# New constants in the scheduler's account of latencies, and new marks per score tile, in a fused attention and GLU kernel

## The chip, the cores and the metric

The kernel runs on one core of a Trainium2 chip. The metric is the device time of one execution in microseconds (us); lower is better. Durations of single instructions are given in nanoseconds (ns). The engines are PE (TensorE: matrix multiplications, with PEld for its weight loads), DVE (VectorE), ACT (ScalarE), POOL (GpSimd) and SP (SyncE, which issues most DMAs). Each engine has its own list of instructions, and semaphores make it wait for the others.

## What is computed

One transformer block over 2048 tokens of width 512: layer norm, attention with 32 heads of 16 dimensions, a residual, a second layer norm, a gated feed-forward network of inner width 1792, and a second residual. All inputs are bf16.

```python
def _A_ref(x, wqkv, wo):                       # H = 32, Dh = 16, S = 2048, D = 512
    q, k, v = split(x @ wqkv)
    scores = jnp.einsum("bhqd,bhkd->bhqk", q, k) * (Dh ** -0.5)
    p = _softmax(scores, axis=-1)
    o = jnp.einsum("bhqk,bhkd->bhqd", p, v)
    return merge_heads(o) @ wo

def _B_ref(x, w_gate, w_up, w_down):           # F = 1792
    h = _sigmoid(x @ w_gate) * (x @ w_up)
    return h @ w_down

h  = x + _A_ref(_layernorm(x), A_wqkv, A_wo)
h2 = h + _B_ref(_layernorm(h), B_w_gate, B_w_up, B_w_down)
```

## The kernel before

**Three stages.** A prologue (about 21 us) loads x, makes its layer norm and the first keys and queries. The main stage (21 to 753 us) runs attention, and squeezes all the other work that can already be done between the pieces of attention: the remaining projections, the output projection, and the feed-forward network of all token blocks but the last. A tail (753 to 783 us) does the last block's output projection and feed-forward network.

**Score tiles.** Attention is cut into 2048 units: 512 columns of scores for one head and one block of 128 keys. Three units make a tile (the last has two), so there are 683 tiles. For tile `n`, PE writes the transposed scores into one of two PSUM buffers `pss` (line 1119, three matmuls, or six of half the width). ACT turns them into bf16 exponentials in one instruction (`pt`, line 1503). Since there are two `pss` buffers, the scores of tile `n` can't begin before the exponentials of tile `n-2` are finished.

**Splitting a tile.** In many tiles ACT takes only two of the three units (128x1024 instead of 128x1536). DVE takes the third: it writes a 16-bit integer code `J` that, read as bf16, is an approximate exponential (line 1298), and for every four such units makes three shifted codes (`code`, line 1318, 128x2048), whose average is more exact. A unit on ACT is multiplied with the values once. A unit on DVE is multiplied four times, with `J` and with each of its three codes. These products (called AV below) accumulate in `acc` (line 1272); four of them, for four heads, run side by side in four column groups of PE, and such a group of four over 512 columns is called a round.

**Background work.** Everything else on PE is queued in `bg` as generators which each yield a few matmuls (`pe(2)` is two rounds' worth): value, key and query projections (`prep_v`, `prep_k`, `prep_q`), the output projection (`wo_add`), the feed-forward network (`ffn_up`, `ffn_down`). They write the one buffer `pm`, which ACT (`th`, the tanh of the gate, line 983) or DVE (`hT`, line 967, and others) empties before the next step can write it. If nothing fits and PE has done little for a while, `fill` issues a matmul whose result nobody reads (line 712).

**The scheduler.** The order of the main stage is not written out by hand. While the program is built, a loop keeps an account of when each engine will be free (`T["P"]`, `T["A"]`, `T["D"]`, `T["G"]`), and always lets the engine with the earliest time choose its next piece: `pe_step`, `act_step`, `dve_step`, `gps_step`. Each choice adds an assumed cost and notes when others may use the result. These costs are constants: a round on PE 217.5 ns (`MM`), the scores of a tile 214 ns (`SMM`), going into and out of score matmuls 105 and 116 ns (`S_IN`, `S_OUT`), 51 + 426.5 ns per unit on ACT, a hop between engines 100 ns (`LAT`), and a few offsets which tell how much later than its slot a result is complete. Only the order goes into the program: the hardware never sees the constants. It waits for semaphores, so a wrong constant makes no wrong result, only an order whose waits fall elsewhere than the account says.

**Marks.** Three strings of 683 letters (`MARKS`, a letter per tile and engine) bend the rules at single tiles. For ACT, `x` forbids to split this tile, `j` allows more work waiting on DVE, `o` gives DVE the first unit and not the last, `l` lets a group of codes stay open longer. For PE, `w` and `v` allow 150 ns more or less before the next scores, `p` presses AV forward, `f` puts background work first, `r` and `R` change how full AV rounds must be, `a` and `b` take or give credit for background work. For DVE, `s`, `e` and `c` shift its priority between `J`, other jobs, and codes.

In `pe_step`, PE may take AV or background work only while it fits before the next scores are due:

```python
act_end = max(T["A"], last_sc + LAT if e < s else T["A"])
limit = act_end + (s - e) * 905 - 520 if s < N else 1e12
room = limit - t + {"w": 150, "v": -150}.get(way, 0)
```

Of the kernel before, what the change touches and what calls it, by code (L numbers as in the profile page):

```python
# [10 lines left out]
BF16 = mybir.dt.bfloat16  # L11
# [12 lines left out]
CODE_STEP = (55, 93, 24)  # L24
MARKS = {
    "A": (
        "........x.oo.xoxxol....ojjoj.x.ooo....x.x....oxx..........j.jj...........o.x"
        "x.o.......xx.lj.jlljjj.xox..ooxjojj.j..x.j..x..j....ooo..ooooooj.x..jjj.jj.."
        "....jj...jjj...lol.....j..j..o....llll.jl...lll..o..............j..x..xx...."
        "jjjjj.jjjj.j..xxx.....j..o.....x...j.......x.ll..........................llj"  # L30
        "jjjjj.xo...llll.......xxx..j..o.j..............j.j.x.j........x.l..........x"
        "..............jj..xxo.j..oooo.ooo....oo......xooo....l..lllj.....x...l.....x"
        ".....lllllll.j.l.j.......jjjjlllll....xo.....j.jjjjjj.......l..oololoooo.x.x"
        "x..o...llll.x........o.jjjj..........l..........l.ll.lll...lllxljjl...j.jj.."
        "...llllxl..........xxoo....jjjjj.lx....j..........j.jx.xxxxx.o.ooooo.xx...l"
    ),
    "P": (
        "............aRR.ww........vww..p.p.pr........pp......f..ffR..a.a.aa..va..p.p"
        "p....vvvv.vvvbb....v.vf.a.bw........................f......p.p...vvvvvv.pvbb"
        ".b...........b.b.a...R.ppp.bR.r....b........pRRp.p..............wRRR.vvvvrr."  # L40
        "...rrp............f.br.v.vvvvv....pf........f....bb.....bb.bb..appp.aaa..pR."
        "aRp.a..v.v...p............wbww.wp.f......v.vvRv.vv.R.vpv..f.ffffafpp........"
        ".v.........RR...........RR..w...fff.ffv....p..........pvp..r..pprwrvr..brr.R"
        "Rrr.p.........f..aaaaaa..vvv...........vv..fvvvvr....f...f.ff.rpp...R......."
        "...............rrr...RR.ffR........brp.....ff...vvv.vvvv.w....v.wwp.....pp.p"
        ".r.......ab..a..pppwb..p...rf...........pffrr.R......rfffv.RRf.r...w...frrr"
    ),
    "D": (
        "....c..................cc...ee....s..........................c..c..........."
        ".c..sssssss..eeeeeee..e...ss..ssss..................c...c.e.ss.............."  # L50
        "....c.s........c.eec.ssss..........ccsssss.ss...ss................e........."
        ".....c.ccscc.....cccsssc.ecc.c.........c.......ee...eeeee.eee..ss..........."
        "....................e.................s.........eeee..s..............cc.scc."
        "........c......ee.ee......c.e...c...........cc......eeee...........sc......."
        "........es...................................c...sss.e.......c.............."
        "c............ssssss...........eeeeees..........s..................s.c......."
        "....s.......e.c.c.c.c.......ee....................c.....ss.sc..........c..."
    ),
}

# [1 line left out]
def kernel(  # L62
# [12 lines left out]
    P = 128  # L75
    S, D = A_x.shape[1], A_x.shape[2]
# [200 lines left out]
    V, A, E = nc.vector, nc.scalar, nc.tensor  # L277
# [132 lines left out]
    def center0(key, a, b, out):  # L410
# [5 lines left out]
        out=small.tile([P, 1], FP32, name="warm")[:], in_=eps_t[:], func=ACT.Sqrt))])  # L416
# [8 lines left out]
    for c in range(NQC):  # L425
# [40 lines left out]
        out=small.tile([P, 1], FP32, name="warm")[:], in_=eps_t[:], func=ACT.Exp))])  # L466

    def qproj0():
# [39 lines left out]
    while left:  # L508
        best = None
        for n in left:  # L510
            t = tasks[n]
# [20 lines left out]
        t = tasks[n]  # L532
# [155 lines left out]
                        moved = True  # L688

    MM = 217.5  # L690
    SMM, S_OUT, S_IN = 214.0, 116.0, 105.0
    FILL = 2000.0
    SPAN = 3413.0
    FROOM = 200
# [358 lines left out]
    def try_bg(tokens, loose=60.0):  # L1053
        while bg and bg[0][2] is None:
            advance()
        if not bg:
            return 0
        ns, mm, deps, mode = bg[0][2]
        ends = [d.end for d in deps if d is not None]
        if None in ends:  # L1060
            return 0
        r = max(ends, default=-LAT) + LAT
        if mm == 0:
            st["mark"] = None
            advance()
            return try_bg(tokens, loose)
        if tokens < mm or r > T["P"] + loose:
            return 0
        T["P"] = max(T["P"] + switch(mode), r) + ns
        st["work"] = "b"  # L1070
        worked(ns)
        st["mark"] = Mark(T["P"])
        bg[0][3] -= mm
        advance()
        return mm
# [32 lines left out]
    def scores(n):  # L1108
        for k in queries(n):
            force(k)  # L1110
        pss = ps_s.tile([P, GU, QC], FP32, name="pss")
        first = True
        for a in range(2):
            for ui, (q, g, kt, j) in enumerate(tiles[n]):
                hg = head_groups(q, g)
                if a >= len(hg):
                    continue
                w = QC // len(hg)
                mm = nc.tensor.matmul(  # L1119
                    pss[:, ui, a * w:(a + 1) * w],  # L1120
                    lhsT=KT[hg[a]][32 * j:32 * j + 32, kt * P:(kt + 1) * P],
                    rhs=(QT0[q] if q < NQC and g == 0 else QT[hg[a]])[32 * j:32 * j + 32, columns(q, a)],
                    start=True, stop=True, tile_position=(32 * j, 0))
# [26 lines left out]
    def finish_group(q, g):  # L1150
# [29 lines left out]
        def turn():  # L1180
# [111 lines left out]
    def dexp_first(src, un):  # L1292
        if not half:
            half.append(dvx.tile([P, NJ, QC], U16, name="J", bufs=NJB))
            first_codes.append([1])
        J, held = half[0], first_codes[-1]
        k = len(half) - 1
        first = nc.vector.tensor_scalar(out=J[:, k, :], in0=src, scalar1=128 * SC * LOG2E,  # L1298
                                        scalar2=float(CODE_BASE), op0=ALU.mult, op1=ALU.add)
        half.append(un)  # L1300
        held[0] += 1
        avq.append(Unit(un.u, J[:, k, :].bitcast(BF16), un.n, T["D"] + 680, held))
        prior["op"] = J
        if k == NJ - 1:
            dexp_rest()
        return first

    def dexp_rest():
        J, uns = half[0], half[1:]
        half.clear()  # L1310
        k = len(uns)
        j = J[:, 0:k, :]
        mine = first_codes[-1]
        mine[0] += NCODE - 1

        def code(i):
            c = dvx.tile([P, NJ, QC], U16, name="code", bufs=CB)[:, 0:k, :]
            nc.vector.tensor_scalar(out=c, in0=j, scalar1=CODE_STEP[i], scalar2=None, op0=ALU.add)  # L1318
# [138 lines left out]
    def act_step():  # L1457
# [24 lines left out]
        if (len(tl) == GU and len(jq) < 2 and mark("A", n) != "x"  # L1482
# [12 lines left out]
            elif can and back <= EASY:  # L1495
# [6 lines left out]
        pt = ptp.tile([P, GU, QC], BF16, name="pt")  # L1502
        ex = nc.scalar.activation(out=pt[:, lo:lo + wa, :], in_=pss[:, lo:lo + wa, :],  # L1503
                                  func=ACT.Exp, scale=SC)
# [198 lines left out]
```

## Time and profile before

| | us |
|---|---|
| median of three runs (lowest, highest) | 785.53 (784.61, 785.80) |
| the profiled execution's own time | 784.84 |
| its span, from first to last instruction | 782.8 |
| first and last start of an exponential (line 1503) | 21.0 and 751.6 |
| PE busy, PEld busy | 756.6 and 374.8 |
| ACT busy | 755.1 |
| DVE busy | 720.3 |
| PE clock granted | 1.000 throughout |

Two things need care when these are read. A busy share counts the time in which at least one instruction of the engine was in flight. Instructions of one engine overlap: an exponential of two units lasts 1018 ns or more from its start to its end, but when ACT is fed well the next one starts 904 ns after it. Short waits thus vanish under the overlap, and ACT at 100% busy in the main stage may still be waiting. The distance from one start to the next shows them; sums below are therefore made of such distances and not of durations. And the median of the runs lies 0.69 us above the profiled execution.

### The profile page before, as it was taken

The numbers are of one execution on the slowest core, as the hardware profiler recorded it, in microseconds if no ns is written. First come the engines' busy times: TensorE is split into PE (matmuls) and PEld (weight loads), VectorE is DVE, ScalarE is ACT, GpSimd is POOL, SyncE is SP. The second block draws the span as 40 slices with busy tenths as digits, with TensorE's granted clock in tenths as the row PEclk, the third lists the DMA queues.
The fourth block names the chain that finished last, engine by engine and source line by source line (L and its number), as shares of the span: only waits on it lengthen the run. The fifth ranks groups of instructions, "written<-read, shape, count | busy, mean of one in ns | idle before, by whom it ended". The sixth has DMA issues, their size and how long they took to land.

```text
span 782.8 us, 34032 instructions
## 1 busy us (share of the span) xinstructions
PE 756.6 (97%) x15274; PEld 374.8 (48%) x15274; DVE 720.3 (92%) x1339; ACT 755.1 (96%) x786; POOL 47.4 (6%) x124
## 2 busy tenths in 40 slices
PE   8999999999999999999999999999999999999998
PEld 7423323444455534554455434554554355544656
DVE  6999999999999999999998999999999999999652
ACT  7999999999999999999999999999999999999972
POOL 2000000000110001000100001001000010000000
PEclk9999999999999999999999999999999999999999
DMA  6503022236013320221023310320133113223510
GB/s 200 122 2 76 2 50 48 58 72 179 16 30 82 85 63 15 71 84 57 15 58 90 90 43 26 109 82 11 37 97 90 56 41 92 84 63 102 155 34 21
DMA packets 93810, 52.99 MB, mean 68 GB/s; under 512 B 21520, under 2 KB 92576, under 8 KB 93664
## 3 DMA queue, kind: packets, MB, share of 16 engines
q1 hardware_dynamic: 92848, 50.56, 23.5%
q8 instruction: 119, 1.95, 1.0%
q10 hardware_dynamic: 816, 0.26, 0.1%
q14 instruction: 27, 0.22, 0.1%
HBM read 39.52 MB, written 2.11 MB: 53 GB/s over the span
## 4 chain that ended last, share of the span: by engine, by line
ACT 42%; PE 30%; issue 13%; DVE 12%; POOL 1%; DMA 1%; SPq 0%; ACTq 0%; DVEq 0%
ACT pt L1503 40%; PE pm L214 10%; PE acc L1272 8%; PE pss L1119 8%; DVE J L1298 5%; DVE code L1318 4%; ACT th L983 2%; PE gu L209 2%; PE hp L1673 1%; DMA code<-in_A_x_dram 1%; DVE qd L815 0%; DVE xs L1205 0%; PE acc L209 0%; DVE ob L977 0%; DVE h L932 0%
## 5 line engine op out<-in xcount | busy, mean ns | idle before, releaser
L1503 ACT ACTIVATE pt<-pss 128x1024 bf16<-128x1024 f32 (+1 forms) x683 | 716.7, 1212 | 1.8 <-PE pss L1119 1.1
L1298 DVE TENSOR_SCALAR J<-pss 128x512 uint16<-128x512 f32 x501 | 332.2, 681 | 10.4 <-PE pss L1119 9.8
L1119 PE MATMUL pss<-QT,KT 32*128 32x256 bf16 (+1 forms) x3584 | 269.3, 288 | 16.3 <-ACT pt L1503 10.7
L1318 DVE TENSOR_SCALAR code<-J 128x2048 uint16<-128x2048 uint16 (+3 forms) x399 | 249.9, 658 | 0.7
L1272 PE MATMUL acc<-pt,Vaug 128*17 128x256 bf16 (+1 forms) x2701 | 233.6, 290 | 0.3
L1272 PE MATMUL acc<-code,Vaug 128*17 128x256 bf16 (+1 forms) x2649 | 197.2, 288 | 0.1
L1119 PEld LDWEIGHTS <-KT 32*128 32x128 bf16 x3584 | 89.3, 92 | 209.2 <-issue 109.1
L1272 PEld LDWEIGHTS <-Vaug 128*17 128x17 bf16 x6233 | 137.4, 90 | 101.3 <-issue 81.6
L1272 PE MATMUL acc<-J,Vaug 128*17 128x256 bf16 (+1 forms) x883 | 144.0, 288 | 0.1
L214 PE MATMUL pm<-xT,wgu 128*32 128x256 bf16 x3136 | 116.2, 274 | 1.1 <-DMA wgu<-in_B_w_gate_dram 0.4
L214 PEld LDWEIGHTS <-wgu 128*32 128x32 bf16 x3136 | 76.6, 96 | 27.0 <-issue 23.8
L214 PE MATMUL pm<-wd,hT 128*32 128x512 bf16 x728 | 53.2, 383 | 0.3 <-DVE h L932 0.3
L967 DVE SCALAR_TENSOR_TENSOR hT<-th,pm 128x512 bf16<-128x512 f32 x49 | 33.3, 680 | 13.2 <-PE pm L214 12.7
L1171 POOL TENSOR_TENSOR o<-xs,rec 128x256 bf16<-128x256 f32 x23 | 16.2, 706 | 391.9 <-DVE rec L1167 391.9
L983 ACT ACTIVATE th<-pm 128x512 f32<-128x512 f32 x49 | 33.6, 685 | 0.0
L1205 DVE STREAM_TRANSPOSE xs<-acc 128x512 f32<-128x512 f32 x32 | 22.7, 711 | 6.0 <-PE acc L1272 5.8
L214 PEld LDWEIGHTS <-hT 128*32 128x32 bf16 x728 | 14.3, 95 | 17.8 <-issue 13.4
L214 PE MATMUL pm<-xT,wk_sb 128*32 128x512 bf16 x256 | 19.5, 383 | 0.1
L214 PE MATMUL pm<-xT,wq_sb 128*32 128x512 bf16 x256 | 19.5, 383 | 0.1
L214 PE MATMUL pm<-wo_sb,ot 128*32 128x512 bf16 x224 | 17.3, 383 | 0.7 <-DVE hT L967 0.5
L214 PE MATMUL pm<-wv_sb,xT 128*32 128x448 bf16 x256 | 17.5, 356 | 0.0
L1177 POOL TENSOR_TENSOR o<-xs,rec 128x256 bf16<-128x256 f32 x8 | 5.3, 660 | 187.3 <-DVE rec L1167 187.3
(155 smaller groups left out, 347.4 us busy)
## 6 DMA issues: line engine op xcount, KB each, us to landing
wgu<-in_B_w_gate_dram SPq DMA_DIRECT2D x49, 256.0 KB
wgu<-in_B_w_up_dram SPq DMA_DIRECT2D x49, 256.0 KB
KT<-half_neg SPq DMA_DIRECT2D x7, 512.0 KB
QT<-qd SPq DMA_DIRECT2D x28, 128.0 KB
KT<-kd SPq DMA_DIRECT2D x7, 256.0 KB
wd<-in_B_w_down_dram SPq DMA_DIRECT2D x1, 1792.0 KB
xr<-in_A_x_dram SPq DMA_DIRECT2D x14, 128.0 KB
out_dram<-ob SPq DMA_DIRECT2D x14, 128.0 KB
```

What stands on the lines that cost most here:

```text
L209: nc.tensor.matmul(ps, lhsT=lhsT, rhs=rhs, start=start, stop=stop)
L214: nc.tensor.matmul(ps[r, :], lhsT=lhsT[:, r], rhs=rhs, start=start, stop=stop, tile_position=(0, 32 * j), skip_group_check=True)
L967: nc.vector.scalar_tensor_tensor(out=hT[:, 2 * k:2 * k + 2, :].rearrange("p f q -> p (f q)"), in0=th[:], scalar=1.0, in1=ps, op0=ALU.add, ...
L983: nc.scalar.activation(out=th[:], in_=ps, func=ACT.Tanh, scale=0.5)
L1119: mm = nc.tensor.matmul(pss[:, ui, a * w:(a + 1) * w], lhsT=KT[hg[a]][32 * j:32 * j + 32, kt * P:(kt + 1) * P], rhs=(QT0[q] if q < NQC and ...
L1171: V.tensor_tensor(out=o2[:, 0:NB, :].rearrange("p b (a d) -> p a b d", a=2), in0=xs[:, :, 0:DH].rearrange("p (a b) d -> p a b d", a=2), in ...
L1205: j = st["acc"] = dve(630, lambda: nc.vector.transpose(out=xs[:].rearrange("p b r -> p (b r)"), in_=acc[:]), Mark(T["P"]))
L1272: nc.tensor.matmul(acc[32 * j:32 * j + VW, a * w:(a + 1) * w], lhsT=Vaug[:, kt, 4 * hg[a] + j, :], rhs=un.ap[:, a * w:(a + 1) * w], start= ...
L1298: first = nc.vector.tensor_scalar(out=J[:, k, :], in0=src, scalar1=128 * SC * LOG2E, scalar2=float(CODE_BASE), op0=ALU.mult, op1=ALU.add)
L1318: nc.vector.tensor_scalar(out=c, in0=j, scalar1=CODE_STEP[i], scalar2=None, op0=ALU.add)
L1503: ex = nc.scalar.activation(out=pt[:, lo:lo + wa, :], in_=pss[:, lo:lo + wa, :], func=ACT.Exp, scale=SC)
L1673: nc.tensor.matmul(ps, lhsT=hT[:, f, i * P:(i + 1) * P], rhs=wd[:, f, a:b], start=apart and f == 0, stop=(f == FC - 1), skip_group_check=True)
```

## The change

Two parts. The first replaces constants of the account:

- `S_OUT` and `S_IN` go from 116 and 105 ns to 113 and 97.
- The scores of a tile are held to be complete 185 ns after PE's slot, not 165 (`sc_end`).
- The exponentials are held to be complete 66 ns after ACT's slot, not 31, and ACT's slot is 16 ns longer when ACT had to wait.
- Results of background matmuls and of `acc` are held to be complete 115 or 175 ns after PE's slot, where nothing was added before (`st["mark"]`, and the transposition of `acc`).
- `J` is held to be complete 40 ns earlier than before, and a code 35 ns earlier.

The second replaces the three strings of marks: 322 of 683 letters differ for ACT, 352 for PE, 160 for DVE. The kernel's functions, tiles, buffers and formulas stay as they are; what the program executes changes only through the order that the scheduler now chooses, and through which tiles it splits.

```diff
 MARKS = {
     "A": (
-        "........x.oo.xoxxol....ojjoj.x.ooo....x.x....oxx..........j.jj...........o.x"
+        ".....xjj.jo..xoxxooo.oo.jjoj.x.o..x..xooo.....xx.....ooo....jj.......l...j.x"
...
     "P": (
-        "............aRR.ww........vww..p.p.pr........pp......f..ffR..a.a.aa..va..p.p"
+        ".......ff...vRR.ww........vww..p..a..RRR....p......v.a.vaafffa.wpa....a...ww"
...
     "D": (
-        "....c..................cc...ee....s..........................c..c..........."
+        "...e.e...........cc....cc...ee..........c......ce.c..........c..c..........."
...
-    SMM, S_OUT, S_IN = 214.0, 116.0, 105.0
+    SMM, S_OUT, S_IN = 214.0, 113.0, 97.0
...
-        st["mark"] = Mark(T["P"])
+        st["mark"] = Mark(T["P"] + (175 if bg[0][1][0] in ("f", "ln") else 115))
...
-        sc_end[n] = T["P"] + 165
+        sc_end[n] = T["P"] + 185
...
         j = st["acc"] = dve(630, lambda: nc.vector.transpose(
-            out=xs[:].rearrange("p b r -> p (b r)"), in_=acc[:]), Mark(T["P"]))
+            out=xs[:].rearrange("p b r -> p (b r)"), in_=acc[:]), Mark(T["P"] + 175))
...
-        avq.append(Unit(un.u, J[:, k, :].bitcast(BF16), un.n, T["D"] + 680, held))
+        avq.append(Unit(un.u, J[:, k, :].bitcast(BF16), un.n, T["D"] + 640, held))
...
-            avq.extend(Unit(un.u, c[:, m, :].bitcast(BF16), un.n, T["D"] + 85, held)
+            avq.extend(Unit(un.u, c[:, m, :].bitcast(BF16), un.n, T["D"] + 50, held)
                        for m, un in enumerate(uns))
...
-        T["A"] = start + 51 + 426.5 * wa
-        uns = [Unit(u, pt[:, ui, :], n, T["A"] + 31) for ui, u in enumerate(tl)]
+        T["A"] = start + 51 + 426.5 * wa + 16 * (start > t)
+        uns = [Unit(u, pt[:, ui, :], n, T["A"] + 66) for ui, u in enumerate(tl)]
         if split:
             jq.append((n, pss[:, pick, :], uns.pop(pick), ex))
         else:
-                    ex_end[n] = T["A"] + 31
+                    ex_end[n] = T["A"] + 66
```

More of the change, by code (lines that the diff above doesn't have):

```diff
@@ L26 @@
     "A": (
-        "........x.oo.xoxxol....ojjoj.x.ooo....x.x....oxx..........j.jj...........o.x"
[L28 to L32, printed above, removed]
@@ L33 @@
-        ".....lllllll.j.l.j.......jjjjlllll....xo.....j.jjjjjj.......l..oololoooo.x.x"
-        "x..o...llll.x........o.jjjj..........l..........l.ll.lll...lllxljjl...j.jj.."
-        "...llllxl..........xxoo....jjjjj.lx....j..........j.jx.xxxxx.o.ooooo.xx...l"
+        ".....xjj.jo..xoxxooo.oo.jjoj.x.o..x..xooo.....xx.....ooo....jj.......l...j.x"
+        "..oloooooooox..jj..jjjjjox..xxxxoxjlooojoj...x.lllll.ll..jx...ljooo.jjl.ll.."
+        "x...ll.jj..............jjllll..j..oxll.jl...lllj.j........x.oooljj..jjjjl..."
@@ new lines @@
+        "jjjjj.jjjj.j..xxx.o..lllj.jjjjjjxxjj.......x.ll..l...o.x......x..o.oo...l.lo"
+        "ooooooo.....lll...xo.o.oo.o.l.......olll.lox....l..x.j..l....ox.l.l........o"
+        "..xjl.........jjl.jj.j...oj...xo..ooo...ool..joool..xlllloo.o.o.l.llol...jj."
+        "o..oo...llll.j.l.lxl.oj.xxjjj..lll.....x.....xx....jjl.ll.jjj..ojj.....o...x"
+        "x......l.......ooooo.lljljx.oj....xll.....jj.j.jj..j.jjjj.llllxl.jl..jjoo..."
+        ".......oooooooojjo.xxoo.jj.jjjjj.l..ox.ll...j.l........ojjj.jjjjo.oo.x.x..."
@@ L36 @@
     ),
     "P": (
-        "............aRR.ww........vww..p.p.pr........pp......f..ffR..a.a.aa..va..p.p"
[L39 to L43, printed above, removed]
@@ L44 @@
-        "Rrr.p.........f..aaaaaa..vvv...........vv..fvvvvr....f...f.ff.rpp...R......."
-        "...............rrr...RR.ffR........brp.....ff...vvv.vvvv.w....v.wwp.....pp.p"
-        ".r.......ab..a..pppwb..p...rf...........pffrr.R......rfffv.RRf.r...w...frrr"
+        ".......ff...vRR.ww........vww..p..a..RRR....p......v.a.vaafffa.wpa....a...ww"
+        "wwwwwfvvaa.vpppp.vv.R.RfR.brrRr....rr.p.....ffffff.rrrr..rrpR.p....aa.a.aaav"
+        "pb...RR.b.b..b.b.p...R......vrRrRw.pp.vv....vRfvrpp...........bbRR.Rva.vvr.f"
@@ new lines @@
+        "f.rr.......vvv....fpbr.vvvvvv.v..rpf........r.r..bb...wpww.bb.ppaaw.pRR..pf."
+        "....fpp.prR.......R.ffww.pb..v..p.f......vrrrrv..www.v.v..f....vvvvvvbRR..aw"
+        "wwwff.ff...vv..p............wva...wwwfRrbbvb......p........r..fvvvpva.r...aa"
+        "....pv.....wpppp...p.r...vpv............aw.bbww..w...f..f.ppp.......R.R.aa.b"
+        "b.f.rrrrrrrv...rw.w.www..p....a..a...aav....ff...ffr.aa....rppv.ffff.bf....."
+        "vv..r....a.Rvvv.vvp.pbb.R.v.v......r........RRv..rr..rfff..a..a...vv...frrr"
@@ L47 @@
     ),
     "D": (
-        "....c..................cc...ee....s..........................c..c..........."
[L50 to L54, printed above, removed]
@@ L55 @@
-        "........es...................................c...sss.e.......c.............."
-        "c............ssssss...........eeeeees..........s..................s.c......."
-        "....s.......e.c.c.c.c.......ee....................c.....ss.sc..........c..."
+        "...e.e...........cc....cc...ee..........c......ce.c..........c..c..........."
+        ".c..s.ssssseee.e..ceeeee.ees..sseee........e.eeeeee.cee.........s..........."
+        "...sc.s........c.e.....s...........ccsssss.ss...ss...........c.cc.ccc......."
@@ new lines @@
+        ".....c.ccscc..eee........e.c.c.........c..eee..c.ccc..ceeeeee..c.....c.....e"
+        "ee.ee..c.c........e.e.....c.cc....................ece.s..............ce.scc."
+        ".s......c......e.cce......c.e.e.c.ccc.e.....c.c.c.e.ee.ce...cc......c......."
+        "......ccc...cccc..c....e.............ee......e...............c.......s......"
+        "c............cessss..eeecc....eee.ees.e........s.s................s.c......."
+        "....scccc...e.......c.......ee.c..........e.......c..ccccccs...sse.....c..."
```

## The prediction

> **What bounds the kernel now.** I read the page's busy times first, then the groups by form, then the timeline of single engines.
>
> ```profile
> PE 756.6 (97%) x15274; PEld 374.8 (48%) x15274; DVE 720.3 (92%) x1339; ACT 755.1 (96%) x786; POOL 47.4 (6%) x124
> PEclk9999999999999999999999999999999999999999
> ACT 42%; PE 30%; issue 13%; DVE 12%; POOL 1%; DMA 1%; SPq 0%; ACTq 0%; DVEq 0%
> ```
>
> Three engines are nearly full, and the chain of waits changes hands between ACT and PE. Which of them sets the pace must be read from distances between starts.
>
> ```profile
> L1503 ACT ACTIVATE pt<-pss 128x1024 bf16<-128x1024 f32 x502 | 489.1, 1101 | 1.7 <-PE pss L1119 1.1
> L1298 DVE TENSOR_SCALAR J<-pss 128x512 uint16<-128x512 f32 x501 | 332.2, 681 | 10.4 <-PE pss L1119 9.8
> L1503 ACT ACTIVATE pt<-pss 128x1536 bf16<-128x1536 f32 x181 | 263.5, 1520 | 0.0
> L1318 DVE TENSOR_SCALAR code<-J 128x2048 uint16<-128x2048 uint16 x354 | 233.2, 689 | 0.6
> L1119 PEld LDWEIGHTS <-KT 32*128 32x128 bf16 x3584 | 89.3, 92 | 209.2 <-issue 109.1 <-DVE J L1298 67.9 <-DVE code L1318 7.7
> ```
>
> 502 tiles are split and 181 are not. The means (1101, 1520 ns) contain overlap and waits; ACT's timeline gives the net times (start, length, instruction, count):
>
> ```profile
> 729.09 0.61 ACT L983 ACTIVATE th<-pm 128x512 f32<-128x512 f32 x1
> 729.58 4.15 ACT L1503 ACTIVATE pt<-pss 128x1536 bf16<-128x1536 f32 x3
> 733.57 0.65 ACT L983 ACTIVATE th<-pm 128x512 f32<-128x512 f32 x1
> ...
> 738.69 4.95 ACT L1503 ACTIVATE pt<-pss 128x1024 bf16<-128x1024 f32 x5
> 743.51 0.62 ACT L983 ACTIVATE th<-pm 128x512 f32<-128x512 f32 x1
> 743.99 4.66 ACT L1503 ACTIVATE pt<-pss 128x1024 bf16<-128x1024 f32 x4
> 748.45 0.69 ACT L983 ACTIVATE th<-pm 128x512 f32<-128x512 f32 x1
> ```
>
> Three unsplit tiles from 729.58 to 733.57 are 1.330 us each. The four from 743.99 to 748.45 are two unsplit and two split ones (the merged row names the first form only): (4.46 - 2.66)/2 = 0.90, and the commonest distance behind a split tile is 0.904. A tanh takes 0.477. Five split tiles should take 4.52 us from 738.69, but the tanh behind them starts 4.82 later: 0.30 us of waiting that no idle column shows. PE shows why:
>
> ```profile
> 737.67 0.39 PE L1119 MATMUL pss<-QT,KT 32*128 32x256 bf16 x6
> ...
> 738.54 0.39 PE L1119 MATMUL pss<-QT,KT 32*128 32x256 bf16 x6
> ...
> 739.30 1.05 PE L214 MATMUL pm<-xT,wgu 128*32 128x256 bf16 x30
> 740.28 0.39 PE L1119 MATMUL pss<-QT,KT 32*128 32x256 bf16 x6
> ```
>
> From one tile's scores to the next PE needs 0.436 us plus 0.2175 for each round: 0.87 with two rounds (737.67 to 738.54), 1.74 with six (738.54 to 740.28). Six rounds in one go outlast the buffer of two tiles.
>
> The main stage from the first exponential at 21.0 to the end of the last at 752.7 is 731.7 us. ACT's net work is 502 x 0.904 + 181 x 1.330 + 49 x 0.477 = 717.9, so it waits 13.7 us. Single distances put 11.5 us of that into 83 waits of over 50 ns, and in all but seven of these the scores came late because PE was still busy, not because DVE still read the buffer. Up to tile 200 PE has room: 191 us of work against ACT's 207, with 3.1 us of waits. From there to the last scores ACT has 509.7, PE 477 x 0.436 + 5 x 0.218 (scores following scores directly) + 1339 rounds x 0.2175 = 500.3, with 10.4 of waits. So ACT sets the pace, with PE 1.9% behind it.
>
> **The change part by part.** I compared the two built orders, instruction by instruction.
>
> *ACT.* 508 tiles are split instead of 502. Each further split takes 1.330 - 0.904 = 0.426 us from ACT: 6 x 0.426 = -2.56 us. By stretch: tiles 0 to 199 lose one split (+0.43), the rest gain seven (-2.98), four of them in the last 33 tiles. There DVE has room: the unsplit run at 729 to 738 shows its `hT` step idle before it for 3.83 us.
>
> *DVE.* Six more `J` at 0.600 (start to start in a queue), six more codes of 128x2048 at 0.600, three fewer of 128x1536 at 0.466, three more of 128x512 at 0.201: +6.4 us. Its net work in the main stage is some 690 of 731, so 34 us of cover remain, and I count 0. Without the cover a late `J` holds the next scores but one. The worst place is tiles 50 to 99, where DVE's net work rises from 51.3 to 53.1 us against ACT's 50.7 plus 0.9 of waits: at most +1.5.
>
> *PE.* A unit moved to DVE costs three more products: 36 half-width matmuls, 4.5 rounds if packed by four. The new order packs worse: 962 AV rounds before the last scores instead of 950. With two more background rounds before tile 200 and as many fewer later, two more fills, and nine direct score-to-score pairs instead of five, PE's work from tile 200 on is 501.8 (+1.5) while ACT's is 506.8 (-3.0). PE's room there shrinks from 9.4 to 5.0 us. What that costs: waits per tile were 15 ns where room was 80 ns a tile, and 22 where it was 19.5; along this line room of 10 gives 23, which is +0.5 us over 482 tiles. The other end is that PE sets the pace and all 4.4 us of lost room come back as waits. I take +0.5, since even the tightest stretches of 50 tiles (room about 0) show only 1.2 us of waits, against 0.8 in the four roomy ones.
>
> *The constants.* They move no instruction by themselves, only the order. The loop that matters is exponential, next scores, next exponential. Read off single instructions: the end of a split tile's exponential lies 114 ns behind the slot of 904, the first score matmul follows 50 after that end, the exponential that waits for it 490 after that matmul: 654. The old account said 31 + 100 + 214 + 165 + 100 = 610, the new one says 665. The old one thus planned arrivals that were 44 ns late in truth; if all 83 large waits shrink by that much, the gain is 3.7 us. The other way: for scores with both switches the new account says 214 + 113 + 97 = 424, the old one 435, the trace 436. The new order believes PE 12 ns a tile faster than it is, up to 482 x 0.012 = 5.8 us where PE sets the pace. Most of what that loss could be already stands in the shrunken room. I take -1.0 for the loop, nearer to nothing than to its end, because most large waits are over 100 ns and come from lumps such as the one above: single gaps whose PE work exceeds what two tiles of ACT can cover are 15 in the old order and 9 in the new, but over runs of four gaps there are 65 and 69.
>
> *Queues.* On SP one pair of `wgu` loads (0.37 and 0.50 us to issue) moves ahead of four loads of late weights into `KT`, which wait for scores; those weights are first read behind 760, and the `wgu` wait of 0.7 us at 731.9 delays no exponential. On POOL one normalisation (0.7 us) moves ahead of four Newton steps; POOL is 6% busy. After the last scores 22 half-width AV matmuls remain instead of 32 (0.27 us), but the last exponential's end sets that moment. All 0; if the cover were gone, -0.3 to +0.7 together.
>
> Sum: -2.56 + 0.5 - 1.0 = -3.1 us on the profiled 784.84, thus 781.8. The median lies 0.69 higher, so the forecast is 782.5.
>
> [...]
>
> **The rivals.**
>
> *PE takes over.* For: from tile 200 on PE's room is only 1% in the new order, three stretches of 50 tiles (from 300, 450 and 550) have more work on PE than on ACT, and the account flatters PE's switches. Against: 9.4 us of room became 10.4 us of waits, not more, in the old order. It decides once PE's lateness is carried from tile to tile. Price: +0.43 on ACT before tile 200, -3.0 on ACT and +4.4 of waits after it, and no gain in the loop gives 787.4.
>
> *Nothing comes through.* Waits grow by what ACT saves, as reshuffled lumps fall less well: 13.7 becomes 16.3, and the time is 785.5. For: 834 letters changed, so every large wait of the old order is dealt anew. Against: fewer single lumps.
>
> *PE has room and the loop is right.* The whole 3.7 us and the 2.56 come through, nothing is lost on PE: 779.3. [...] Against: the room counted above.
>
> **How the numbers follow.** Forecast 0.46, PE takes over 0.27, nothing comes through 0.15, full gain 0.12. The forecast's own range is 780.5 to 785 (waits 1 to 2.5 us off). The range 778.8 to 788 takes in all cases. About 0.2%, 1.6 us, is what can be told from no change: faster means below 784.0. Faster: 0.46 x 0.88 + 0.12 = 0.52. Same: 0.46 x 0.12 + 0.12 of the third case + 0.03 of PE taking over = 0.21. Slower: 0.27.
>
> **What would show it.** Right: split tiles 508, ACT's net work 715.4, and waits in the distances of 12 to 14 us, still mostly from PE; the stretch from 721 to 740 without long unsplit runs. Loop step right: waits between 50 and 100 ns (30 of the 83) become rare. Wrong: waits over 16 us, crowded in tiles 300 to 349, 450 to 499 and 550 to 599 (PE took over), or scores that start just as a `J` ends around tiles 50 to 99 (DVE).

## The result, and the profile after

The changed kernel takes 783.16 us (median of 9 runs, 782.80 to 784.36), beside 784.77 us (9 runs, 784.53 to 785.80) for the kernel before on the same chip. The ratio is 0.9979, with a 95% interval of 0.9970 to 0.9987: faster by some 0.2%, as forecast in sign, with 782.5 forecast and 783.16 measured. A second series (experiment 11 below) gave 783.00 and a ratio of 0.9971 (0.9960 to 0.9981).

The profiled execution of the changed kernel is the slowest of its nine, 784.36 us with a span of 782.6. Its page:

```profile
PE 756.3 (97%) x15312; PEld 374.1 (48%) x15312; DVE 728.6 (93%) x1351; ACT 753.4 (96%) x786; POOL 50.1 (6%) x124
PEclk9999999999999999999999999999999999999999
PE 39%; ACT 32%; DVE 15%; issue 11%; DMA 1%; SPq 1%; POOL 0%; ACTq 0%; DVEq 0%
```

The busy shares hardly moved. The chain of waits did: it now runs over PE for 39% of the span and over ACT for 32%, where it was 30% and 42% (40% and 32% in a second profile of the changed kernel, experiment 11). The groups by form:

```profile
L1503 ACT ACTIVATE pt<-pss 128x1024 bf16<-128x1024 f32 x508 | 495.3, 1092 | 3.0 <-PE pss L1119 2.1 <-ACT pt L1503 0.3
L1503 ACT ACTIVATE pt<-pss 128x1536 bf16<-128x1536 f32 x175 | 253.6, 1512 | 0.1
L1318 DVE TENSOR_SCALAR code<-J 128x2048 uint16<-128x2048 uint16 x360 | 239.5, 695 | 0.5
```

508 tiles are split and 175 are not, so ACT's net work is 508 x 0.904 + 175 x 1.330 + 49 x 0.477 = 715.4 us, 2.56 less than before. ACT's timeline at the end of the main stage (start, length, instruction, count) shows where four of the six further splits went:

```profile
729.33 3.82 ACT L1503 ACTIVATE pt<-pss 128x1024 bf16<-128x1024 f32 x4
733.20 0.60 ACT L983 ACTIVATE th<-pm 128x512 f32<-128x512 f32 x1
733.69 4.71 ACT L1503 ACTIVATE pt<-pss 128x1024 bf16<-128x1024 f32 x5
738.27 0.62 ACT L983 ACTIVATE th<-pm 128x512 f32<-128x512 f32 x1
```

Nine split tiles now stand where the kernel before had seven from 729.58 to 738.21, four of them unsplit. The four from 729.33 take 3.87 us to the next tanh, 0.25 more than 4 x 0.904.

**A stretch at half clock.** The page's clock row hides something, because one digit averages 19.6 us. Three windows around the start of the main stage (stretch, its length, then busy us and count of PE, PEld, DVE, ACT and POOL, the granted clock, the DMA share and GB/s):

```profile
17.06:20.47 3.41, 1.87 (x19) 1.20 (x18) 2.45 (x10) 2.44 (x5) 0.41 (x2) 1.00 0.03 7
20.47:23.90 3.43, 3.20 (x28) 1.97 (x28) 2.26 (x5) 1.94 (x2) 0.00 (x0) 0.50 0.70 180
23.90:27.00 3.10, 2.51 (x32) 1.34 (x27) 3.01 (x7) 2.90 (x4) 0.00 (x0) 1.00 1.06 324
```

For 3.4 us PE ran at half its clock. It is no property of one kernel: of the 59 executions of the kernel before that ran beside the experiments, 13 have a granted clock of 0.997 or 0.998 on record and take 785.67 us in the median, the other 46 take 784.76. The profile of the kernel before has no such stretch there, so the two profiles can't be subtracted without care; experiment 11 gave one of the same kernel without it. The time by stretch, from those two undisturbed profiles (us; distances between starts of exponentials, and waits as such distances less ACT's net work):

| stretch | before | changed | difference | of it ACT's net work | of it waits |
|---|---|---|---|---|---|
| start to first exponential | 21.00 | 20.46 | -0.54 | | |
| tiles 0 to 199 | 210.30 | 210.92 | +0.62 | +0.43 | +0.19 |
| tiles 200 to 649 | 481.86 | 481.27 | -0.59 | -1.28 | +0.69 |
| tiles 650 to 682 | 38.43 | 36.96 | -1.47 | -1.70 | +0.23 |
| last exponential's start to the end | 31.20 | 31.17 | -0.03 | | |
| span | 782.79 | 780.78 | -2.01 | -2.56 | +1.11 |

The main stage became 1.44 us shorter (the medians of the two series fell by 1.6 and 2.2 us). What ACT saved in tiles 0 to 649 (0.85) went into waits again (0.88). The gain is that of the last 33 tiles, 1.47 us; between tiles 660 and 670 alone it is 2.24, of which the next twelve tiles, with more split tiles in the old order, give some back. The 0.54 us at the start is not the change's: the first exponential began between 20.41 and 21.76 us in profiles of kernels whose prologue is the same.

### The profile page after: what moved, and what is told of

It is laid out like the page before. It is cut to its first block, busy times and chain, and to the rows that moved or that the text cites. A ratio compares the mean times of both kernels' runs of the same rounds, so it can differ in the third digit from the quotient of the medians.

```text
span 782.6 us, 34120 instructions
## 1 busy us (share of the span) xinstructions
PE 756.3 (97%) x15312; PEld 374.1 (48%) x15312; DVE 728.6 (93%) x1351; ACT 753.4 (96%) x786; POOL 50.1 (6%) x124
## 4 chain that ended last, share of the span: by engine, by line
PE 39%; ACT 32%; DVE 15%; issue 11%; DMA 1%; SPq 1%; POOL 0%; ACTq 0%; DVEq 0%
ACT pt L1503 31%; PE pm L214 12%; PE acc L1272 11%; PE pss L1119 11%; DVE J L1298 7%; DVE code L1318 5%; PE gu L209 2%; ACT th L983 1%; DMA code<-in_A_x_dram 1%; DVE qd L815 1%; PE hp L1673 1%; DVE hT L967 1%; DVE xs L1205 0%; PE acc L209 0%; DVE h L932 0%
## 5 line engine op out<-in xcount | busy, mean ns | idle before, releaser
L1298 DVE TENSOR_SCALAR J<-pss 128x512 uint16<-128x512 f32 x507 | 337.8, 683 | 12.2 <-PE pss L1119 10.3
L1318 DVE TENSOR_SCALAR code<-J 128x2048 uint16<-128x2048 uint16 (+3 forms) x405 | 254.3, 662 | 0.6
L1272 PE MATMUL acc<-pt,Vaug 128*17 128x256 bf16 (+1 forms) x2689 | 229.8, 290 | 0.0
L1272 PE MATMUL acc<-code,Vaug 128*17 128x256 bf16 (+1 forms) x2685 | 199.7, 288 | 0.2
L1119 PEld LDWEIGHTS <-KT 32*128 32x128 bf16 x3584 | 87.5, 92 | 212.4 <-issue 114.1
L1272 PE MATMUL acc<-J,Vaug 128*17 128x256 bf16 (+1 forms) x895 | 141.8, 288 | 0.0
L983 ACT ACTIVATE th<-pm 128x512 f32<-128x512 f32 x49 | 31.9, 651 | 0.0
L214 PEld LDWEIGHTS <-hT 128*32 128x32 bf16 x728 | 14.5, 95 | 17.0 <-issue 13.2
L214 PE MATMUL pm<-xT,wk_sb 128*32 128x512 bf16 x256 | 19.9, 383 | 0.0
```

The lines of the kernel that those rows point to most:

```text
L214: nc.tensor.matmul(ps[r, :], lhsT=lhsT[:, r], rhs=rhs, start=start, stop=stop, tile_position=(0, 32 * j), skip_group_check=True)
L983: nc.scalar.activation(out=th[:], in_=ps, func=ACT.Tanh, scale=0.5)
L1119: mm = nc.tensor.matmul(pss[:, ui, a * w:(a + 1) * w], lhsT=KT[hg[a]][32 * j:32 * j + 32, kt * P:(kt + 1) * P], rhs=(QT0[q] if q < NQC and ...
L1272: nc.tensor.matmul(acc[32 * j:32 * j + VW, a * w:(a + 1) * w], lhsT=Vaug[:, kt, 4 * hg[a] + j, :], rhs=un.ap[:, a * w:(a + 1) * w], start= ...
```

## The experiments

The theory was the prediction's: ACT sets the pace, a split tile saves 0.426 us, PE's smaller room costs some of it, and the truer constants save waits. The rivals: the gain is the late splits and nothing else; the constants do all or nothing; PE's room costs everything or nothing.

**1 and 2: the late unsplit tiles.** In the order before, the six `x` marks at tiles 661 and 663 to 667 were freed (four more splits, ACT's net work 715.7 by the built order); in the changed order they were put back (four fewer).

```diff
 (1: strings and constants of before, end of the ACT string)
-        "...llllxl..........xxoo....jjjjj.lx....j..........j.jx.xxxxx.o.ooooo.xx...l"
+        "...llllxl..........xxoo....jjjjj.lx....j..........j.j........o.ooooo.xx...l"
 (2: the changed kernel, end of the ACT string)
-        ".......oooooooojjo.xxoo.jj.jjjjj.l..ox.ll...j.l........ojjj.jjjjo.oo.x.x..."
+        ".......oooooooojjo.xxoo.jj.jjjjj.l..ox.ll...j.l......x.xxxxxjjjjo.oo.x.x..."
```

> The kernel before with six letters changed: the marks that forbid to split tiles 661 and 663 to 667 are taken away, all else as before (the order is the same up to tile 660). 506 tiles are split instead of 502. Tail theory: the whole gain of the change comes from the last 33 tiles, which cost ACT 1.7 us less there; so this gains 1.4 to 1.8 us on the kernel before, as much as the change. Spread theory (the better account pays off everywhere): at most 0.4 us of gain here. PE theory: PE has no room there either, and the four splits gain under 0.5 us.

> The changed kernel with the opposite edit: the marks at tiles 661 to 667 forbid to split, where the old strings had it, all else as changed. 504 splits instead of 508, ACT 1.7 us more in the last 33 tiles. Tail theory: the time goes back to that of the kernel before, within 0.5 us. Spread theory: at least 1 us faster than the kernel before.

Measured: 786.20 us for the first (ratio 1.0014, 1.0005 to 1.0023, against 784.89 before) and 784.53 for the second (0.9996, 0.9988 to 1.0005). So in the new order the four splits are worth about 1.4 us (784.53 against 783.16), of 4 x 0.426 = 1.70; with them gone the gain is gone, as the tail theory had it. In the old order the same splits lose 1.3 us, where that theory expected a gain of 1.4 to 1.8. The main stage did get shorter, from 731.7 us (first start to last end of an exponential) to 749.69 - 20.41 = 729.3. But after the last exponential 34.2 us were left in place of 30.05. PE's timeline of that kernel shows why (start, length, instruction, count, idle time before it and what ended it):

```profile
750.23 1.06 PE L214 MATMUL pm<-xT,wgu 128*32 128x256 bf16 x32 [0.72 <-ACT th L983]
752.14 1.48 PE L214 MATMUL pm<-wd,hT 128*32 128x512 bf16 x24 [0.86 <-DVE hT L967]
753.44 0.62 PE L1272 MATMUL acc<-pt,Vaug 128*17 128x256 bf16 x10
```

A gate step and an up step no longer fitted ahead of the last scores. Now they stand alone at the end of the main stage, where PE waits first for the tanh of the gate (0.72 us) and then for `hT` (0.86) with nothing to fill the gaps. The unsplit tiles of the old order were not idle for PE: there it did background work, and it was DVE that rested. The old order from 729.58 to 738.21 (the columns are those of the windows above):

```profile
729.58:738.21 8.63, 7.55 (x199) 4.97 (x200) 3.87 (x7) 8.63 (x10) 0.04 (x1) 1.00 0.54 156
```

And the changed one over the nine tiles now in that place, in the undisturbed profile of experiment 11:

```profile
727.51:736.45 8.94, 8.72 (x240) 5.26 (x238) 8.94 (x17) 8.90 (x12) 0.62 (x1) 1.00 0.75 222
```

DVE's 3.87 us of 8.63 became 8.94 of 8.94, PE's 7.55 became 8.72, and as before 56 matmuls of queued background work (512 columns each) are left behind the last scores. The new order does this stretch's background work in time beside the splits; the old one, given the same splits, does not.

**3 and 4: each half of the change alone.** New constants with the old strings, and the new strings with the old constants.

```diff
 (3: the strings of before with)
+    SMM, S_OUT, S_IN = 214.0, 113.0, 97.0
+        sc_end[n] = T["P"] + 185
...
 (4: the new strings with)
+    SMM, S_OUT, S_IN = 214.0, 116.0, 105.0
+        sc_end[n] = T["P"] + 165
...
```

> The new constants with the old marks. 496 splits, ACT's net work 720.5 (2.6 more than before), PE's about 6 us more, single gaps with too much PE work 25 instead of 15. If marks only fit the account that they were found under: 3 to 6 us slower than before. If the better account is worth something by itself: no slower than before.

> The old constants with the new marks. 502 splits, six of them more in the last 33 tiles and six fewer between tiles 200 and 650; single gaps with too much PE work 31 instead of 15. If marks only fit their own account: 1 to 4 us slower than before, the tail's gain of about 2 us included. If the marks alone carry the gain: as fast as the change.

Measured: 793.91 (1.0111, 1.0095 to 1.0126) and 804.57 (1.0245, 1.0231 to 1.0259). Both are worse than either whole, by far more than the 3 to 6 and 1 to 4 us that were expected. With the constants alone only 496 tiles are split (ACT's net work 720.5) and 21.8 us are waited for, against 13.6 before; single gaps whose PE work exceeds what two tiles of ACT can cover number 25 by the built order, against 15 before and 9 after. With the strings alone they number 31 and the waits come to 28.8 us, and one accident costs most:

```profile
157.82 0.40 PE L1272 MATMUL acc<-code,Vaug 128*17 128x256 bf16 x8 [0.21 <-DVE code L1318]
161.47 0.40 PE L1119 MATMUL pss<-QT,KT 32*128 32x256 bf16 x3 [3.25 <-DMA QT<-qd]
```

The next queries reach `QT` 3.25 us late, and PE's granted clock is 0.50 for the 6.8 us from 160.05 to 166.90. From tile 100 to tile 150 this kernel takes 11.5 us longer than the kernel before. Neither run says what the constants are worth by themselves.

**5 and 6: the same constants, half a nanosecond off.** To see how far an order depends on its exact account, `SMM` was raised by 0.2%, in the kernel before and in the changed one.

```diff
-    SMM, S_OUT, S_IN = 214.0, 116.0, 105.0
+    SMM, S_OUT, S_IN = 214.5, 116.0, 105.0
```

> A control: the kernel before with the constant for a tile's scores at 214.5 ns instead of 214.0, a difference that no trace could tell. The order is the same up to tile 154, then 487 tiles are split instead of 502 (ACT's net work +5.9 us), and a full feed-forward step (64 matmuls) stays behind for the tail. If marks fit only the very order that they were found in: 6 to 11 us slower than before. If orders of the same account are all about alike: within 2 us.

> The same control on the changed kernel: 214.5 ns instead of 214.0. 505 splits instead of 508 (ACT +1.2 us), single gaps with too much PE work 12 instead of 9. If marks fit only their own order: 2 to 6 us slower than the changed kernel. If the better account makes orders robust: within 1.5 us of it, so 783 to 784.7.

Measured: 799.47 for the kernel before (1.0192, 1.0164 to 1.0219) and 789.59 for the changed one (1.0054, 1.0039 to 1.0069, so 6.4 us over itself). Half a nanosecond in an assumed cost, which the program doesn't even contain, costs 14.5 and 6.4 us, more than any term of the prediction's sum. The split tiles fall to 487 and 505, the granted clock is 0.994 and 0.993 in the two profiles (estimated from their spans of 801.5 and 787.6 us: some 10 and 11 us at half clock), and in the first 64 more matmuls are left for the tail. The profile of the first (its slowest execution, 803.53 us) is 18.7 us longer than that of the kernel before: 5.9 of ACT's net work, 6.0 of waits, and 6.7 behind the last exponential. In these two orders a string of marks fits one exact account: taken with another, however little other, its letters hit the wrong situations. Experiments 3 and 4 fit that reading, but changed too much at once to show it.

**7 and 8: PE lighter, the order untouched.** In the main stage's gate and up steps half of the contraction is left out, which takes 42.6 us from PE (an estimate: 392 chunks over 256 columns, each at 0.109 us, half the round of 0.2175) and changes no other engine's work.

```diff
-        for d in range(DC):
+        n = DC // 2 if mm is quarters else DC
+        for d in range(n):
             mm(ps[:, f * HQ:(f + 1) * HQ], w[:, d, f * P:(f + 1) * P], hnT[:, d, :],
-               d == 0, d == DC - 1)
+               d == 0, d == n - 1)
```

> The kernel before, same order, but half of the contraction of gate and up projection left out in the main stage (two of four chunks in each of the 196 products of 256 columns), so that PE's work is 42.6 us less there, spread from tile 200 on, and ACT's the same. PE theory (waits of ACT come from lumps of PE work): the 10.4 us of waits after tile 200 shrink to 3 to 5, and the time to 777 to 780. If the waits are hops between engines that PE's work doesn't change: 783 or more.

> The changed kernel with the same half of the contraction left out. With PE out of the way ACT's net work alone should tell: 2.6 us below the light version of the kernel before, against 1.6 between the full ones, if PE's smaller room costs the change 1 us. If PE's room costs it nothing, the gap stays 1.6.

Measured: 785.42 from the kernel before (1.0007, 0.9996 to 1.0018) and 781.66 from the changed one (0.9953, 0.9938 to 0.9968). With 5.6% less PE work, one kernel is no faster and the other by 1.5 us. Over tiles 200 to 649 the waits are 9.31 us in both, where they were 9.92 and 10.61. The shrinking to 3 to 5 us that the PE theory of experiment 7 expected did not come, yet the waits are not hops between engines either. Of the 84 single waits of over 50 ns in the kernel before (83 by the prediction's count), 73 (10.4 us) come with scores that PE's own work held up, as do 63 of 73 with the lighter PE; but only 15 of those 73 (2.4 us) have a gate or up step just ahead of the scores. Most of what remains has nothing to do with gate and up steps. The wait of 0.266 us at tile 486, in the kernel before:

```profile
535.97 0.39 PE L1119 MATMUL pss<-QT,KT 32*128 32x256 bf16 x6
536.29 1.05 PE L214 MATMUL pm<-wd,hT 128*32 128x512 bf16 x16
537.27 0.39 PE L1119 MATMUL pss<-QT,KT 32*128 32x256 bf16 x6
```

and the same with the lighter PE (its lines are numbered one higher, and it runs 0.7 us earlier):

```profile
535.22 0.40 PE L1120 MATMUL pss<-QT,KT 32*128 32x256 bf16 x6
535.55 1.05 PE L214 MATMUL pm<-wd,hT 128*32 128x512 bf16 x16
536.53 0.39 PE L1120 MATMUL pss<-QT,KT 32*128 32x256 bf16 x6
```

1.30 and 1.31 us from scores to scores, one down step between them, and the same wait. Such lumps of AV rounds and other background work cost the same here with 42 us more of room. With the lighter PE the kernel before also ran for a while at half clock (windows as above, from that run):

```profile
732.10:735.50 3.40, 2.06 (x48) 1.26 (x45) 1.46 (x3) 3.40 (x5) 0.00 (x0) 1.00 0.22 60
735.50:742.30 6.80, 6.74 (x98) 2.68 (x97) 5.28 (x9) 5.30 (x7) 0.00 (x0) 0.50 0.27 79
```

In its unsplit stretch PE was busy for only 2.06 of 3.40 us, then had half its clock for 6.8, and three exponentials waited 2.3 us. Without that, its waits from tile 200 on would be 9.6 us, against 9.5 for the changed order. From the first to the last start of an exponential the two light kernels are 4.67 us apart; less those 2.3 it is 2.4, near the 2.6 that experiment 8 expected if PE's load is what costs the change its 1 us.

**9 and 10: PE heavier, the order untouched.** The first contraction chunk is done twice in the first half of each gate step and of each up step: 98 x 0.109 = 10.7 us more for PE by the same estimate, nearly all of it after tile 200 (the first gate step's tanh starts at 226.8, and tile 200's exponential at 231.3, so 0.2 to 0.4 us lie ahead).

```diff
-        for d in range(DC):
+        for d in ([0] if mm is quarters and f == 0 else []) + list(range(DC)):
```

> The kernel before, order untouched, but in the main stage each half of a gate or up step repeats its first contraction chunk, so PE has 49 x 2 x 0.109 = 10.7 us more of work between tiles 0 and 682 (the repeated chunk starts the accumulation anew, so the result is the same). Theory A, PE's total room sets the waits (what the prediction's rival 'PE takes over' used): the room from tile 200 on falls from 9.4 us to about 2, and by the prediction's line (23 ns of waits per tile at 10 ns of room) the time rises by 1 to 3 us, to about 786 to 788. Theory B, waits come from single lumps of work between two scores, whatever the total: only gaps that hold a gate or up step and were already full get longer, some 98 steps by up to 0.109 us each, but most of them have slack: under +1.5 us, to 785 to 786.5.

> The same repeated chunk (PE + 10.7 us) in the kernel after. Theory A: the room from tile 200 on, 5.0 us, turns to about -2.5 and the lack comes out as time: + 4 to 6 us on the kernel after, to 787 to 789, and so clearly more than the kernel before loses by the same. Theory B: about the same small loss as the kernel before, under +1.5, to 783 to 784.7.

Measured: 790.19 (1.0066, 1.0050 to 1.0083) and 791.82 (1.0082, 1.0067 to 1.0098), beside 785.18 before and 783.00 for the changed kernel in the same series. The kernel before loses 5.0 us, the changed one 8.8. Theory B's bound of 1.5 falls; theory A has the order right and both sizes too small (it took the room left for 2 and -2.5 us; the prediction's count less 10.7 gives -1.3 and -5.7). Where the extra waits stand tells more than either. After tile 200 the single waits of over 50 ns grew by 4.2 us in the kernel before, 3.6 of it at scores with a gate or up step just ahead, and by 7.9 in the changed one, 6.3 of it there and 1.7 behind AV rounds. So theory B had the place right and the size wrong: there a third of the added work was paid for in the one order and some 0.6 of it in the other, which also passed a part on. The changed order, 1.6 to 2.2 us ahead, ends 1.6 behind. ACT's timeline over five split tiles that took 4.58 us in experiment 11:

```profile
731.87 4.71 ACT L1503 ACTIVATE pt<-pss 128x1024 bf16<-128x1024 f32 x5
736.45 0.62 ACT L983 ACTIVATE th<-pm 128x512 f32<-128x512 f32 x1
```

With the heavier PE:

```profile
738.52 1.02 ACT L1503 ACTIVATE pt<-pss 128x1024 bf16<-128x1024 f32 x1
739.85 1.02 ACT L1503 ACTIVATE pt<-pss 128x1024 bf16<-128x1024 f32 x1 [0.31 <-PE pss L1119]
741.34 2.88 ACT L1503 ACTIVATE pt<-pss 128x1024 bf16<-128x1024 f32 x3 [0.47 <-PE pss L1119]
744.12 0.59 ACT L983 ACTIVATE th<-pm 128x512 f32<-128x512 f32 x1
```

The same five take 5.60 us, and the waits are now long enough to appear as idle time before the second and the third.

**11: the changed kernel again, nothing edited.**

> The kernel after, unchanged, for more runs and another profile. Theory (half-clock window): PE's half clock of 3.4 us at the start of the main stage in the first profile is chance, and cost about 1.05 us. If so a profile without it has its first exponentials within 0.4 us of those of the kernel before up to tile 12, a span near 781.5, and waits near 14.0 us in place of 15.1; the median stays at 782.8 to 783.5 and the ratio at 0.997 to 0.9985. If the window comes back in the profile, it belongs to this order.

Measured: 783.00 us (8 runs), ratio 0.9971 (0.9960 to 0.9981), span 780.8, no half-clock stretch in the main stage, waits 14.7 in place of 15.6. At tile 50 this profile is 1.81 us ahead of the first one: 0.89 by its earlier start, 0.92 by the wait at tile 2 that the half clock had made. The expected 1.05 for that stretch was thus about right, and its span was lower than expected by the earlier start.

**12: the heavier PE by half.** The repeated chunk in the gate steps only: 5.3 us more for PE, in the changed kernel.

```diff
-        pair_mm(ps, w[:, 0], 0)
+        pair_mm(ps, w[:, 0], 0, again=(0,))
```

> The kernel after with the repeated first chunk only in the gate half of each step: 196 more matmuls, PE + 5.3 us, all after tile 200, the result the same. Theory (the price of PE work follows its room, as a curve through all kernels so far: waits per tile after tile 200 of 21.6 ns at 9.4 us of room, 23 at 5.0, 30 at -1.3, 38 at -5.7): the room becomes -0.3, so waits of 28 to 30 ns per tile, 13.5 to 14.5 us after tile 200 in place of 11.2, a span of 783.2 to 784.2 and a median of 785.3 to 786.5, about that of the kernel before. Rival (the price is a fixed share, the 0.69 that the whole 10.7 us cost): 14.8 us of waits, span 784.6 or more.

Measured: 786.23 us (1.0018, 1.0008 to 1.0027), span 784.3, 14.5 us of waits after tile 200 by the total of distances (13.5 by the list of single waits from which the expectation was made). By that list the rival's fixed share, 14.8, is too dear, and the curve's 13.5 to 14.5 holds at its edge; by distances the first 5.3 us of PE work cost 3.0 us of waits and the second 4.9, so the price does bend; the span is just above its range, 0.45 us of it by a later start than in experiment 11. All seven kernels whose orders are one of the two, by PE's room from tile 200 on (counted as in the prediction, changed by all that the edit adds or takes, though up to 0.4 us of the additions and 1.1 us of what is taken lie ahead of tile 200):

| kernel | PE's room, us | waits, us | ns per tile |
|---|---|---|---|
| before, PE lighter (without its half-clock waits) | 52 | 9.6 | 19.9 |
| changed, PE lighter | 47.6 | 9.5 | 19.8 |
| before | 9.4 | 10.5 | 21.9 |
| changed (11) | 5.0 | 11.5 | 23.8 |
| changed, + 5.3 | -0.3 | 14.5 | 30.0 |
| before, + 10.7 | -1.3 | 15.4 | 32.0 |
| changed, + 10.7 | -5.7 | 19.4 | 40.2 |

As far as seven points can tell, both orders lie on one curve: at -1.3 us of room, the line between the changed order's -0.3 and -5.7 gives 15.4 us of waits, which is what the kernel before has. About 20 ns a tile remain even with some 50 us of room. A microsecond of lost room costs 0.2 us of time between 9.4 and 5.0 (from one order to the other), 0.6 from there to nothing, and 0.9 beyond (in the changed order alone).

## Why the prediction was right, point by point

**ACT, -2.56: right.** Splits, net work and place were as counted (the 13.7 us of waits beside it should read 13.8, being 731.7 less 717.9; from the first to the last start they are 13.6), and the four late splits were worth 1.4 of 1.70 us when taken away alone (experiment 2). What the prediction did not say is that DVE's idle time was no sufficient reason to split there: PE's unfinished background work had to be out of the way first (experiment 1).

**DVE, 0: right.** Waits in which the scores came late because a `J` still read the buffer went from 7 (0.81 us) to 2 (0.34), and the waits of tiles 50 to 99, 0.84 us, became 0.73, though DVE is busy for 8 us more.

**PE's smaller room, +0.5: the mechanism right, the size small.** The waits after tile 200 grew by 0.9 us, to 23.8 ns a tile where the prediction's line had 23. That PE's load makes the difference is shown by the runs that changed PE alone: over tiles 200 to 649 the two orders wait equally with a light PE (9.31 and 9.31), 0.69 apart as they are, and 2.35 apart with the heavy one (14.06 and 16.41). That it acts as total room, and not as the slack of single gaps that were already full, is not shown; the places of the extra waits in experiments 9 and 10 speak for the single gaps.

**The constants' loop, -1.0: wrong.** The step that failed is that the old account "planned arrivals that were 44 ns late in truth" and that large waits shrink by this. Waits of 50 to 100 ns, which were to become rare, went from 30 to 31 (experiment 11), and with a light PE, where nothing else could hide such a gain, the new order waits no less than the old. What stands in its place: the waits come from lumps of PE work in the order, 83 of the 90 single waits of over 50 ns in experiment 11, and which lumps an order has is settled by marks and account together. The count of single overfull gaps, 15 and 9, is not their measure, since the waits grew while it fell; over runs of four gaps the prediction's own count rose, from 65 to 69. Whether truer constants help a search to find better marks was not tried; the runs only show that a change of 0.2% in one constant, made afterwards, costs 6 to 15 us.

**Queues and tail, 0: right.** From the last exponential's end to the end of the span 30.05 us became 30.09.

**The sum.** -3.1 was forecast inside the kernel, -1.44 came (-2.56 of ACT, +1.11 of waits). The forecast of 782.5 was nearer than that, because it added 0.69 us for the median of the three runs shown of the kernel before. Its later medians, over 9 to 21 runs each, were 784.77 to 785.18, so most of those 0.69 us were those three runs' chance, and this error covered part of the other. From a median of 784.77 the same -3.1 would have given 781.7, 1.5 us too low, so the closeness of the forecast is partly luck.

**The rivals.** "PE takes over" decides from the point that it named, lateness carried from tile to tile, but the changed order is not there: it has 5.0 us of room, and pays 0.2 us per lost microsecond. Experiment 10, with -5.7, is there, and pays 0.9. "Nothing comes through" is what happened in tiles 0 to 649, though not behind them. "PE has room and the loop is right" fell: with 1.4% more PE work the time rose by 0.6% in the kernel before and 1.1% in the changed one, while the weight loads were busy for 48% of the span in all four. So that 48% told nothing of PE's room here; the distances between score matmuls (0.436 us and 0.2175 a round), with the added rounds, are the measure that held.

## What to carry to other kernels

Where two engines carry nearly the same load, count the room of the one that doesn't set the pace in each stretch and expect a price that bends: in this kernel work on the second engine was almost free above 2% of room (0.02 us per microsecond between 52 us of room and 9.4) and cost nearly its full length at none (0.9), while a floor of some 20 ns of waits a tile stayed at 47.6 and 52 us of room. Look also where the work lands: most of the price was paid at the gaps that the added work made longer. Moving work off the pacing engine at the end of a stage paid here only where the work that its slack was hiding was done elsewhere in time. And these two orders belong to the exact account under which their marks were found: test such a change whole, by the built order's counts and by the clock, and don't credit its parts.

## What the runs showed of the hardware that was not expected

PE's clock fell to half although PE was far from idle. In the changed kernel's first profile PE had been busy for 1.87 of 3.41 us just before, in experiment 7 for 2.06 of 3.40, in experiment 4 for 1.00 of 3.05; the granted clock was then 0.50 for 3.4, 6.8 and 6.8 us, and the waits made in it cost 0.9 us, 2.3 us and a part of 11.5 us.

How busy PE was just before doesn't settle it alone. At the same place in the program, around the first scores, the clock held at 1.00 after less. The kernel before (windows as above):

```profile
17.06:20.47 3.41, 1.74 (x17) 1.22 (x16) 2.45 (x8) 2.30 (x5) 0.41 (x2) 1.00 0.03 7
20.47:23.90 3.43, 2.65 (x32) 1.48 (x32) 3.33 (x8) 2.90 (x4) 0.00 (x0) 1.00 0.62 172
```

And the changed one in experiment 11:

```profile
16.60:20.00 3.40, 1.65 (x16) 1.22 (x16) 2.41 (x8) 2.22 (x5) 0.39 (x2) 1.00 0.03 7
20.00:23.50 3.50, 2.78 (x35) 1.57 (x34) 3.42 (x7) 3.04 (x4) 0.00 (x0) 1.00 0.70 165
```

These lines don't show what decides between the two. In experiment 7 the lighter PE lost time with its clock, at its tile 673: the kernel before had PE busy for 2.94 of 3.40 us at about that place (731.70 to 735.10) and kept 1.00 there and in the 3.40 us behind. Five of the ten runs with the lighter PE have a granted clock of 0.995 or 0.996 on record, and none of the 59 of the kernel before is under 0.997.
